# Seven half-size products for one more chunk's first product, under a new instruction order

## The chip, the cores and the metric

The kernel runs on one core of a Trainium2 chip. The metric is the device time of one execution in microseconds, and the median of three runs is given.

The names of the engines are those of the profile: PE is TensorE (matmuls; PEld its weight loads), ACT ScalarE, DVE VectorE, POOL GpSimd and SP SyncE.

## The reference

Attention with a causal mask and 16 beacon keys that every query sees, then two dense products with a squared relu between them.

```python
# q, k, v: (8, 8, 576, 64); beacon_k, beacon_v: (8, 8, 16, 64)
k_all = np.concatenate([beacon_k, k], axis=2)
v_all = np.concatenate([beacon_v, v], axis=2)
scores = scale * np.matmul(q, k_all.transpose(0, 1, 3, 2))
causal[:, Nb:] = np.triu(np.ones((S, S), dtype=bool), k=1)
scores = np.where(causal, -1000000000.0, scores)
a = np.exp(scores - scores.max(-1, keepdims=True))
a /= a.sum(-1, keepdims=True) + 1e-09
attn_out = np.matmul(a, v_all)
x = attn_out.transpose(0, 2, 1, 3).reshape(B * S, H * D)   # (4608, 512)
h = x @ w_in                                               # w_in: (512, 2048)
r = np.maximum(h, 0.0)
out = (r * r) @ w_out                                      # w_out: (2048, 512)
```

## The kernel before

**Attention.** It goes batch by batch (8 batches), four pairs of heads each. `qk` operations multiply queries by keys into PSUM (line 680 for batches 2 to 7, 687 for 0 and 1; the two heads of a pair sit on 64 rows each), ACT takes the exponential (792; 709 in batch 0), DVE sets masked places to zero (815), `av` multiplies by the values and a column of ones (837), and DVE divides by the sum (854 and 856) into `xn`, tokens by rows. The result is transposed into `xT`, a ring of 1728 tokens, by TensorE (905) for batches 0 to 2 and by DMAs from SP (`xt` operations, line 888, five to a batch) for the others. Keys, queries and values of later batches are loaded by POOL's queue (`ld`, 391; 425 and 445 for queries) and transposed by DMAs from SP (`tr`, 459).

**The dense part.** It goes in 9 chunks of 512 tokens, which don't end where batches do. The first product of a chunk is plain for chunks 0 to 6: for each of 16 tiles of 128 outputs, four matmuls over the 512 inputs (1139), or eight where the chunk crosses the end of the ring. ACT or DVE takes the relu out of PSUM (1154, 1156) and one of them squares (1164, 1166). The second product is plain for chunk 0 (1189) and is made of seven products of half-size blocks for the others (1248), whose sums and differences DVE makes (1220) and whose results are put together on the way out (347, 349, 1271).

**Chunks 7 and 8** make the first product of seven half-size products too (`add_first_both`, line 969). Tokens are split into even and odd, inputs and outputs into halves. POOL copies the chunk out of `xT` (`pull`, by line 349), DVE makes four differences of blocks of x (`xsum`, 996) and once four sums and differences of blocks of `w_in` (`asum`, 963). For each half of the outputs, products 1, 6, 7 and 4 add up in one PSUM strip (the "x" chain); after each of the first three the strip's running sum is copied to a kept area (`hold`, operations `c1`, `u2`, `u3`, by 347), and after the fourth its relu is taken (`c21`, 1038). Products 2, and 5 and 3, go to single PSUM banks in two parts each, and DVE adds the kept sums to them (`plus`, 1063). Then come relus (1087, 1089) and squares (1093, 1095). The kept areas are a pool `held` of five: three lie in the staging area `stg` of the loads, two in the buffer `pt` of attention weights. Chunk 7's copy of x lies in `qk_area`, chunk 8's in `pt`.

**Order.** No scheduler decides the order at run time. `add` registers operations with their dependencies, and `Order.run` issues them in the order of the text SEQUENCE; each word is an operation, with `@A`, `@D` or `@P` where its engine is a choice. Each engine works through its own list in that order, POOL's and SP's DMA issues too. PSUM banks (`ps`, 4), strips (2), kept areas (`held`) and staging areas (`stg`) are handed out in that order as well. `fill` operations are 12 products of an identity matrix (564), whose results nobody reads, spread over the first microseconds.

`s1.j.t.0` is tile t of the plain first product of chunk j, and `s1.j.h.n` product n of half h in the seven-product form; `s2.j.n.t` is part t of product n of the second product. `qk16.2` is a visit of the score products of batch 4, `av15.0.1` the second head of pair 15 (batch 3).

Of the kernel before, what the change touches and what calls it, by code (L numbers as in the profile page):

```python
# [16 lines left out]
ident fldq0 bkl0 fldq1 fldk0 tri fill0 warm fldk1 fill11 fldk2 fldq2 fldk3 bkc0 fldq3 sld0k1.0 tpb0 fill5 ekb0 fck0@A  # L17
fcq0@D fill2 sld0q1.0 bkl1 fcq1@D fill6 sld0k1.2 tp0.0.0k fck1@D fill8 ek0.0.0@A sld0q1.2 fill4 tpg0.0.0k tp0.0.1k
fcq2@A ld0v0 fill9 ek0.0.1@A fck3@D fill3 fck2@D tp0.0.0q tp0.0.1q fill1 eq0.0.0@A fcq3@D ld0v1 eq0.0.1@A tp0.0.3k
tpg0.0.1q tp0.0.3q ek0.0.3@A qk1.0.0 eq0.0.3@A tpg0.0.3k tpg0.0.0q tpg0.0.1k ld0v2 qk0.0.0 tp0.0.2q exp1.0.0 tp0.0.2k  # L20
fill10 two0.1.0k@D two0.1.1k@P eq0.0.2@A qk3.0.0 exp0.0.0 ld0v3 two0.1.1q@D ek0.0.2@A mask0.0.0 tp0.1.1q exp3.0.0
tpg0.0.2k tpg0.0.2q tpg0.0.3q tp0.1.1k mask1.0.0 qk2.0.0 ld0v4 two0.1.0q@D tp0.1.0k ek0.1.1@A eq0.1.1@D tp0.1.0q
exp2.0.0 tpg0.1.1k ek0.1.0@D win0 qk1.1.1 eq0.1.0@A two0.1.3k@D tpg0.1.0k tpg0.1.1q two0.1.2k@D exp1.1.1 mask2.0.0
qk0.1.2 tpg0.1.0q tp0.1.2k win2 two0.1.3q@D fill7 mask3.0.0 exp0.1.2 tp0.1.3q qk0.1.0 bkc1 tp0.1.3k ek0.1.2@D win1
exp0.1.0 qk1.1.0 eq0.1.3@D tpb1 ek0.1.3@D win3 exp1.1.0 tpg0.1.3q av0.0.0 qk0.1.1 ekb1 two0.1.2q@D tpg0.1.3k av1.0.0
norm0.0.0 sld1k0.0 exp0.1.1 qk3.1.0 norm1.0.0 sld1q0.0 xtp0.0.0 av3.0.0 exp3.1.0 qk1.1.2 norm3.0.0 av2.0.0 exp1.1.2
sld1k0.2 norm2.0.0 tp0.1.2q qk3.1.1 mask0.1.1 xte0.0.0@A sld1q0.2 xtp0.0.2 mask0.1.0 qk3.1.2 exp3.1.1 mask1.1.1
av0.1.0 eq0.1.2@D exp3.1.2 mask3.1.1 tpg0.1.2q tpg0.1.2k mask1.1.0 xtp0.0.1 qk2.1.1 xte0.0.1@D ld1v0 xte0.0.2@A
xtp0.0.3 mask3.1.0 qk2.1.0 exp2.1.1 norm0.1.0 av3.1.0 exp2.1.0 qk2.1.2 norm3.1.0 av1.1.0 xte0.0.3@A exp2.1.2 mask2.1.1
mask2.1.0 xtp0.1.3 s1.0.1.0 xte0.1.3@D av2.1.0 norm1.1.0 relu0.1.0@A s1.0.0.0 norm2.1.0 s1.0.10.0 relu0.0.0@A xtp0.1.0  # L30
sq0.0.0@D xtp0.1.2 s1.0.11.0 relu0.10.0@D ld1v1 xte0.1.2@D s1.0.7.0 xte0.1.0@D relu0.11.0@D s1.0.6.0 relu0.7.0@D
xtp0.1.1 s1.0.4.0 relu0.6.0@A xte0.1.1@D s1.0.9.0 relu0.4.0@D s1.0.1.1 relu0.9.0@A ld1v2 sq0.3.0@A s1.0.7.1
relu0.1.1@D s1.0.14.1 relu0.7.1@D s1.0.15.1 relu0.14.1@A s1.0.2.0 ld1v3 two1.0.0k@D s1.0.6.1 relu0.15.1@D relu0.2.0@A
s1.0.13.0 two1.0.1k@D relu0.6.1@A sq0.7.1@D s1.0.12.0 sq0.5.0@A ld1v4 two1.0.0q@D tp1.0.0k relu0.13.0@A relu0.12.0@D
tp1.0.0q ek1.0.0 s1.0.8.0 eq1.0.0@A s1.0.0.1 two1.0.1q@D sq0.3.1@A wout0 tpg1.0.0k tpg1.0.0q qk4.2 two1.0.2k@D
relu0.0.1@A sq0.6.0@D tp1.0.1q relu0.8.0@D exp4.2.0.0.0 s1.0.14.0 eq1.0.1@D s1.0.11.1 wout1 relu0.14.0@A tp1.0.1k
tpg1.0.1q relu0.11.1@A tp1.0.2k exp4.2.1.0.0 ek1.0.1 two1.0.3k@P s1.0.10.1 s1.0.4.1 ek1.0.2 relu0.10.1@A qk4.4 wout2
sq0.5.1@D tpg1.0.2k tpg1.0.1k s1.0.2.1 mask4.0.0 exp4.4.1.0.0 two1.0.2q@P relu0.4.1@D s1.0.8.1 relu0.2.1@D s1.0.3.0
exp4.4.0.0.0 s1.0.9.1 wout3 relu0.3.0@D s1.0.5.1 relu0.9.1@D relu0.8.1@A ldq2.0 s1.0.5.0 sq0.1.0@A mask4.0.1 s1.0.12.1
mask4.0.2 relu0.5.1@A relu0.5.0@D ld2v0 sq0.0.1@A av4.0.0 sq0.2.0@D relu0.12.1@A s1.0.3.1 norm4.0.0 sq0.4.0@A av4.0.1  # L40
two1.0.3q@P relu0.3.1@D tp1.0.2q s1.0.13.1 norm4.0.1 eq1.0.2@A s1.0.15.0 ld2v1 sq0.4.1@D relu0.13.1@A tpg1.0.2q
tp1.0.3k sq0.1.1@A relu0.15.0@D qk5.7 ek1.0.3 ldq2.1 sq0.6.1@A s2.0.0.0 sq0.2.1@D exp5.7.-1.1.0 tpg1.0.3k exp5.7.0.0.0
tp1.0.3q s2.0.2.0 exp5.7.1.0.0 s2.0.0.1 exp5.7.-1.0.0 mask5.0.1 s2.0.2.1 mask5.0.2 eq1.0.3@A mask5.0.0 wsum1 tpg1.0.3q
qk7.13 s2.0.0.2 zero2 exp7.13.-1.1.0 sq0.7.0@A av5.0.0 exp7.13.-1.0.0 ld2k0 s2.0.2.2 norm5.0.0 exp7.13.1.0.0 wsum2
av5.0.1 ld2k1 exp7.13.0.0.0 s2.0.2.3 mask7.0.2 ld2k2 norm5.0.1 s2.0.0.3 join2.1@D qk6.10 zero3 ev0.0@A ev0.2@A
s2.0.1.0 ld2k3 exp6.10.1.0.0 xtp1.0.0 exp6.10.1.0.1 ldq2.r s2.0.1.1 exp6.10.-1.0.0 mask7.0.0 mask7.0.1 exp6.10.-1.1.0
s2.0.3.0 ldq3.0 xte1.0.0@A mask6.0.0 exp6.10.0.0.0 ldq3.1 av7.0.0 s2.0.3.1 ldq3.r mask6.0.1 mask6.0.2 s2.0.1.2
norm7.0.0 ldq4.0 av6.0.0 ld2k4 av7.0.1 norm6.0.0 s2.0.1.3 join2.2@P norm7.0.1 av6.0.1 ldq4.1 join2.3@D xtp1.0.3
norm6.0.1 s2.0.3.2 xte1.0.3@D join3.3@P xtp1.0.2 xtp1.0.1 xte1.0.2@A s2.0.3.3 join3.1@D join2.0@P xte1.0.1@D s1.1.7.0
wsum3 tr2q s1.1.1.0 relu1.7.0@A join3.2@P ev0.3@A s1.1.4.0 relu1.1.0@A wsum4 joined3.1 joined2.0 joined2.1 s1.1.0.0  # L50
relu1.4.0@D s1.1.10.0 join3.0@D tr2k relu1.0.0@D joined3.0 s1.1.6.0 relu1.10.0@D sq1.0.0@A s1.1.5.0 join4.0@D ldq4.r
join4.3@D s1.1.11.0 relu1.5.0@A join4.2@D relu1.6.0@D ldq5.0 s1.1.13.0 relu1.11.0@A sq1.3.0@D ld2v2 s1.1.12.0
sq1.5.0@D relu1.13.0@A ld3k0 s1.1.15.0 qk8.4 relu1.15.0@D ld2v3 s1.1.14.0 relu1.12.0@D exp8.4.0.0.0 ld2v4 s1.1.2.0
sq1.6.0@D exp8.4.1.0.0 ld3k1 relu1.14.0@D relu1.2.0@A qk8.2 sq1.7.0@D ld3k2 s1.1.8.0 sq1.2.0@D exp8.2.0.0.0 ld3k3
s1.1.3.0 sum1.1.1 exp8.2.1.0.0 ld3k4 relu1.8.0@D s1.1.9.0 relu1.3.0@A mask8.0.0 mask8.0.2 qk9.7 mask8.0.1 relu1.9.0@A
sq1.1.0@D ev0.1@A av8.0.0 sq1.4.0@D exp9.7.-1.0.0 st0 s2.1.1.0 exp9.7.-1.1.0 sum1.2.1 st1 exp9.7.0.0.0 av8.0.1
sum1.1.0 tr3q s2.1.2.0 norm8.0.1 exp9.7.1.0.0 exp9.7.1.0.1 norm8.0.0 s2.1.1.1 mask9.0.0 qk10.10 sum1.2.0 ev1.c1.None@A
sum1.3.0 s2.1.2.1 exp10.10.-1.1.0 mask9.0.1 exp10.10.1.0.0 mask9.0.2 s2.1.6.0 tr3k sum1.3.1 ev1.c11.None
exp10.10.0.0.0 av9.0.0 s2.1.6.1 norm9.0.0 mask10.0.1 av9.0.1 ev1.u2.None@A mask10.0.2 xtp2.0.0 norm9.0.1 s2.1.7.0
xte2.0.0@A join5.0@P exp10.10.-1.0.0 qk11.13 ldq5.1 sum1.4.1 mask10.0.0 s2.1.5.0 ldq5.r exp11.13.-1.0.0 sum1.4.0  # L60
exp11.13.0.0.0 av10.0.0 ldq6.0 s2.1.5.1 exp11.13.-1.1.0 ld4k0 exp11.13.1.0.0 mask11.0.0 xtp2.0.1 s2.1.7.1 norm10.0.0
xte2.0.1@A mask11.0.1 ld4k1 qk12.2 mask11.0.2 ev1.u3.None@A av11.0.0 ld4k2 ev1.c22.None exp12.2.1.0.0 av10.0.1
norm11.0.0 s2.1.4.0 ldq6.1 exp12.2.0.0.0 norm10.0.1 ld4k3 av11.0.1 s2.1.3.0 norm11.0.1 ld3v0 xtp2.0.2 xtp2.0.3
xte2.0.2@D s2.1.3.1 xte2.0.3@D ld3v1 s1.2.13.0 ev1.c12.None ld3v2 join4.1@D s1.2.4.0 join5.2@D ld3v3 relu2.13.0@D
# [142 lines left out]
def kernel(  # L207
# [12 lines left out]
    B, H, S, D = q.shape  # L220
# [5 lines left out]
    NT = 5  # L226
# [10 lines left out]
    def sb(name, shape, dt):  # L237
        return pool.tile(shape, dt, name=name)

    FAST = 1  # L240
    BOTH = 7
    NSTG, NPT, RB = 6, 3, 3
    PW = 1664
    RING = RB * S
# [108 lines left out]
    cast = {}  # L353
# [615 lines left out]
    def add_first_both(j, G, sq):  # L969
# [6 lines left out]
        if j == BOTH:  # L976
            add_a_sums()
# [429 lines left out]
```

## Time and profile before

| | |
|---|---|
| Median of three runs | 326.29 us (324.04 to 327.10) |
| The profiled execution | 323.4 us, of which 321.7 us is the span from its first to its last instruction |
| TensorE (PE) busy | 312.7 us, 97% of the span, 3520 matmuls |
| Weight loads (PEld) busy | 230.3 us, 72% |
| DVE, ACT, POOL busy | 240.6 us (75%), 211.4 us (66%), 112.1 us (35%) |
| Plain first products, line 1139 | 640 matmuls, 104.2 us busy |
| Seven-product form of chunks 7 and 8, line 1016 | 224 matmuls of 256 columns |

How to read it: matmuls are pipelined, so a group's mean duration is longer than the time from one start to the next. What a stretch of work costs on TensorE is read from the chain in order of time, which lists the pieces that follow each other without a gap, or from the starts in the timeline. The windows give, for a stretch, the busy time of PE, PEld, DVE, ACT and POOL in this order.

### The profile page before, as it was taken

How to read it: one execution, taken by the hardware profiler on the slowest of the kernel's cores; microseconds unless marked ns; L12 is line 12 of the kernel's file. 1: busy time of each engine (PE TensorE's matmuls, PEld its weight loads, DVE VectorE, ACT ScalarE, POOL GpSimd, SP SyncE). 2: the span in 40 equal slices, each digit the busy share in tenths (PEclk: the TensorE clock that was granted, in tenths of full speed). 3: DMA queues.
4: the chain of work that ended last, by engine and by line, in shares of the span. 5: the costliest groups of instructions: out<-in, count | busy, mean ns of one | idle time of the engine just before them, and what ended most of it. 6: DMA issues, size and time to landing. Idle time of an engine off the chain costs nothing.

```text
span 321.7 us, 8494 instructions
## 1 busy us (share of the span) xinstructions
PE 312.7 (97%) x3520; PEld 230.3 (72%) x3520; DVE 240.6 (75%) x538; ACT 211.4 (66%) x318; POOL 112.1 (35%) x159
## 2 busy tenths in 40 slices
PE   6899999999999999999999999999999999999995
PEld 2468765644886468888786568665887788888884
DVE  3788875688975796856875788778866687989882
ACT  3994987357893787685856685477762686586610
POOL 7934767738089239177440050000000600000000
PEclk9999999999999999999999999999999999999999
DMA  7999999999999999999998989040231600030033
GB/s 156 148 203 200 154 204 149 164 163 137 201 172 155 216 163 149 136 180 120 186 138 144 235 82 163 18 142 3 49 29 30 176 2 0 3 130 2 2 147 114
DMA packets 135934, 39.93 MB, mean 124 GB/s; under 512 B 117336, under 2 KB 131544, under 8 KB 135896
## 3 DMA queue, kind: packets, MB, share of 16 engines
q0 software_dynamic: 84928, 18.10, 73.1%
q1 hardware_dynamic: 50314, 20.93, 30.9%
q8 instruction: 27, 0.44, 0.6%
q10 hardware_dynamic: 654, 0.38, 0.4%
q14 instruction: 11, 0.09, 0.1%
HBM read 37.22 MB, written 9.44 MB: 145 GB/s over the span
## 4 chain that ended last, share of the span: by engine, by line
PE 95%; DVE 2%; ACT 1%; DMA 1%; issue 0%; DVEq 0%; ACTq 0%
PE ps L1139 31%; PE ps L1248 29%; PE ps L837 9%; PE strip L680 5%; PE ps L1189 4%; PE strip L1016 4%; PE ps L1016 3%; PE strip L1248 2%; PE ps L680 2%; PE strip L687 2%; PE ps L905 1%; PE ps L529 1%; PE ps L564 1%; DMA stg<-in_beacon_k_dram 1%; ACT pt L709 0%; DVE g L349 0%
## 5 line engine op out<-in xcount | busy, mean ns | idle before, releaser
L1139 PE MATMUL ps<-xT,w_in 128*128 128x512 bf16 (+6 forms) x640 | 104.2, 315 | 0.0
L1139 PEld LDWEIGHTS <-w_in 128*128 128x128 bf16 x640 | 56.9, 98 | 34.6 <-issue 1.6
L792 ACT ACTIVATE pt<-strip 128x1024 bf16<-128x1024 f32 (+3 forms) x77 | 70.5, 958 | 5.5 <-PE strip L680 5.0
L1154 ACT ACTIVATE g<-ps 128x512 bf16<-128x512 f32 (+2 forms) x77 | 42.1, 558 | 34.8 <-PE ps L1139 32.3
L1248 PEld LDWEIGHTS <-g 128*128 128x128 bf16 x512 | 48.4, 98 | 8.0 <-issue 1.2
L1248 PE MATMUL ps<-w_out,g 128*128 128x256 bf16 x352 | 44.9, 273 | 0.0
L1156 DVE TENSOR_SCALAR g<-ps 128x512 bf16<-128x512 f32 (+2 forms) x51 | 30.2, 603 | 14.1 <-PE ps L1139 13.7
L1248 PEld LDWEIGHTS <-sum_area 128*128 128x128 bf16 x384 | 36.5, 98 | 5.7 <-issue 1.3
L815 DVE TENSOR_TENSOR pt<-pt,tri 128x512 bf16<-128x512 bf16 (+1 forms) x93 | 30.7, 356 | 12.7 <-ACT pt L792 11.3
L837 PEld LDWEIGHTS <-pt 128*128 128x128 bf16 x930 | 35.2, 99 | 6.2 <-issue 1.3
L837 PE MATMUL ps<-vb,pt 128*128 128x65 bf16 x930 | 37.8, 195 | 0.4 <-DVE qT L349 0.4
L391 POOL DMA_DIRECT2D vb<-in_v_dram x40 | 34.2, 876 | 7.5 <-DMA w_in<-in_moe_w_in_dram 6.6
L856 DVE TENSOR_TENSOR xn<-ps,rcp 128x320 bf16<-128x320 f32 (+2 forms) x64 | 31.5, 492 | 2.2
L1166 DVE TENSOR_TENSOR g<-g 128x1024 bf16<-128x1024 bf16 (+2 forms) x42 | 27.2, 662 | 5.6 <-ACT g L1154 5.2
L347 ACT COPY osb<-ps 128x512 f32<-128x512 f32 x27 | 15.7, 587 | 23.4 <-PE ps L1248 21.3
L1248 PE MATMUL ps<-w_sum,sum_area 128*128 128x256 bf16 x240 | 30.8, 273 | 0.2 <-ACT osb L347 0.2
L792 ACT ACTIVATE pt<-ps 128x512 bf16<-128x512 f32 x42 | 24.5, 604 | 8.3 <-PE ps L680 7.6
L391 POOL DMA_DIRECT2D qk_area<-in_k_dram x30 | 25.9, 881 | 4.3 <-DMA w_out<-in_moe_w_out_dram 3.8
L854 DVE RECIPROCAL rcp<-ps 128x5 f32<-128x5 f32 (+2 forms) x64 | 12.1, 189 | 17.8 <-PE ps L837 17.3
L349 POOL COPY qk_area<-xT 128x512 bf16<-128x512 bf16 x4 | 2.8, 747 | 56.4 <-DMA xT<-xn 56.4
L1164 ACT ACTIVATE g<-g 128x1024 bf16<-128x1024 bf16 (+2 forms) x22 | 19.2, 882 | 3.9 <-DVE g L1156 3.7
L1271 DVE TENSOR_TENSOR osb<-ps,osb 128x512 f32<-128x512 f32 (+1 forms) x26 | 16.8, 648 | 6.6 <-PE ps L1248 3.0
(105 smaller groups left out, 421.1 us busy)
## 6 DMA issues: line engine op xcount, KB each, us to landing
out_dram<-osb SPq DMA_DIRECT2D x16, 512.0 KB, 3.3
vb<-in_v_dram POOLq DMA_DIRECT2D x24, 128.0 KB, 5.6
stg<-in_q_dram POOLq DMA_DIRECT2D x12, 256.0 KB, 4.8
qk_area<-in_k_dram POOLq DMA_DIRECT2D x18, 128.0 KB, 5.2
w_in<-in_moe_w_in_dram POOLq DMA_DIRECT2D x4, 512.0 KB, 10.5
w_out<-in_moe_w_out_dram POOLq DMA_DIRECT2D x4, 512.0 KB, 10.3
vb<-in_v_dram POOLq DMA_DIRECT2D x8, 112.0 KB, 6.0
qk_area<-in_k_dram POOLq DMA_DIRECT2D x6, 112.0 KB, 5.0
```

Of the source, the lines that this page charges most:

```text
L391: insts.append(nc.gpsimd.dma_start(out=dst[lo:rows], in_=t[b, :, t0:t0 + rows - lo, :].transpose([1, 0, 2])))
L680: nc.tensor.matmul(out, keys[hp, c, pr], rhs, start=True, stop=True)
L792: nc.scalar.activation(out, in_, AF.Exp, bias=0.0, scale=scale)
L815: nc.vector.tensor_tensor(out=d, in0=d, in1=tri[0:rows, m0:m0 + m, 0:w][:, None].to_broadcast([rows, 2, m, w]), op=ALU.min)
L837: nc.tensor.matmul(a[0:w, at + (t - tl[0]) * (D + 1):at + (t - tl[0] + 1) * (D + 1)], P[0:rr, hj, o:o + w], vb[b % 2][0:rr, c, 2 * pr + hj ...
L856: nc.vector.tensor_tensor(out=xn[b % 2].rearrange("p t (h d) -> p h t d", d=D)[:, h0:h0 + nh, tl[0]:tl[0] + nt], in0=a[:, :, :, 0:D], in1= ...
L1016: nc.tensor.matmul(o[:, i % 2 * HT:(i % 2 + 1) * HT], lhs[:, m, f * 128:(f + 1) * 128], rhs[:, m], start=fresh and i % 2 == 0 and m == 0, ...
L1139: nc.tensor.matmul(h[:, lo - spans[0][0]:hi - spans[0][0]], w_in_sb[:, mc, ft * 128:(ft + 1) * 128], xT[:, mc, lo % RING:lo % RING + hi - lo],
L1154: nc.scalar.activation(dst, h, AF.Relu, bias=0.0, scale=1.0)
L1156: nc.vector.tensor_scalar(out=dst, in0=h, scalar1=0.0, scalar2=None, op0=ALU.max)
L1166: nc.vector.tensor_tensor(out=d, in0=d, in1=d, op=ALU.mult)
L1248: nc.tensor.matmul(o, lhs[:, f, t * 128:(t + 1) * 128], rhs[:, f], start=fresh and f == 0, stop=f == HF - 1, skip_group_check=True)
```

## The change

The first product of chunk 6 takes the seven-product form (`BOTH` from 7 to 6). Chunks 6 and 8 now copy x into `qk_area`, chunk 7 into `pt`. Since batch 7's attention still uses `pt` when chunk 6 begins, an operation without instructions (`grab`) takes the two kept areas in `pt` first, and another (`ptfree`) gives them back after batch 7's last `av`; the first copies wait for the loads that use `stg` (`stg_free`) instead of for attention. In chunk 6 the second half's use of kept areas and banks is tied to the first half's additions (`old`), and the x chain no longer waits for all of batch 7's scores and exponentials. Chunk 6's operations are registered only with the last batch. The whole of SEQUENCE is new, from the first word to the last; the words below show three places of it (the start, the transposes of batch 3 and the copies for chunk 6).

```diff
 SEQUENCE = """
-ident fldq0 bkl0 fldq1 fldk0 tri fill0 warm fldk1 fill11 fldk2 fldq2 fldk3 bkc0 fldq3 sld0k1.0 tpb0 fill5 ekb0 fck0@A
-fcq0@D fill2 sld0q1.0 bkl1 fcq1@D fill6 sld0k1.2 tp0.0.0k fck1@D fill8 ek0.0.0@A sld0q1.2 fill4 tpg0.0.0k tp0.0.1k
+ident fldq0 bkl0 fldq1 fldk0 tri fill10 warm fldk1 fill4 fldk2 fill3 fldq2 fill6 fldk3 fill2 bkc0 fldq3 fcq0@A
+sld0k1.0 fill7 fill1 fck0@D sld0q1.0 tpb0 tp0.0.0q tp0.0.0k sld0k1.2 fill5 eq0.0.0@D fck1@A fcq1@D tpg0.0.0q ek0.0.0@D
...
-mask17.0.0 xt3.2 s2.2.4.0 sum2.4.0 exp16.2.0.0.0 join6.1@D s2.2.5.1 xt3.0 mask16.0.0 mask16.0.1 qk17.8 ev2.c22.None
-xt3.1 s2.2.4.1 exp17.8.-1.1.0 exp17.8.0.0.0 av16.0.0 ev2.c21.None@D tr5q s2.2.3.0 exp17.8.-1.0.0 exp17.8.1.0.0
+joined4.1 joined5.1 join6.0@D av15.0.1 joined6.0 exp16.2.1.0.0 s2.2.5.1 norm15.0.1 mask16.0.0 s2.2.4.0 xt3.3
+mask16.0.1 ev2.c22.None qk17.8 mask17.0.0 xt3.0 s2.2.3.0 exp17.8.-1.0.0 exp17.8.-1.1.0 av16.0.0 xt3.1 exp17.8.0.0.0
+mask17.0.2 s2.2.4.1 norm16.0.0 mask17.0.1 av16.0.1 xt3.2 ev2.c21.None@A av17.0.0 exp17.8.1.0.0 norm16.0.1 s2.2.3.1
...
+norm25.0.0 pull6.1.3072 av25.0.1 mask26.0.1 qk27.13 pull6.0.3072 norm25.0.1 av26.0.0 exp27.13.0.0.0 ld7v0 s2.4.3.1
+norm26.0.0 exp27.13.1.0.0 s2.4.4.1 ev4.c12.None pull6.2.3072 ld7v1 mask27.0.2 s1.5.10.0 mask27.0.1 mask27.0.0
...
 """
...
     FAST = 1
-    BOTH = 7
+    BOTH = 6
...
     order = Order(
-        pools={"strip": range(2), "held": range(5), "ps": range(4), "stg": range(NSTG)},
+        pools={"strip": range(2), "held": (3, 4, 0, 1, 2), "ps": range(4), "stg": range(NSTG)},
     )
...
+    stg_free = []
...
-        exps = [o for q in last for o in qk_ops[q]] + [x[0] for q in last for x in exps_of[q]]
         if j == BOTH:
             add_a_sums()
+            grab = add("grab", "-", 0.0, None, take=("held", 2))
+            add("ptfree", "-", 0.0, None, deps=probs, give=[(grab, 0, "held"), (grab, 1, "held")])
+            stg_free.extend(cast[B - 1, x, c] for x in "qkv" for c in range(NT))
...
+        sums = None
         for half in range(2):
+            old = sums if j == BOTH else None
...
-                        deps=deps + done_g + (exps if chain == "x" else []),
+                        deps=deps + done_g + (old["c11"] if old and chain != "x" else []),
...
-            hold("c1", 1, None, probs)
+            hold("c1", 1, None, stg_free + (old["c11"] if old else []))
...
-            hold("u2", 6, None, [])
+            hold("u2", 6, None, old["c22"] if old else [])
...
-            hold("u3", 7, None, [])
+            hold("u3", 7, None, old["c12"] if old else [])
...
         if b >= 1:
-            for j in late:
-                add_chunk(j)
-            late = []
+            while late and (late[0] < BOTH or b == B - 1):
+                add_chunk(late.pop(0))
```

## The prediction

> **What bounds the kernel now.** I read the page first, then the chain in order of time, the windows, the timelines of TensorE and SyncE, and the rows of single lines.
>
> ```profile
> span 321.7 us, 8494 instructions
> PE 312.7 (97%) x3520; PEld 230.3 (72%) x3520; DVE 240.6 (75%) x538; ACT 211.4 (66%) x318; POOL 112.1 (35%) x159
> ...
> PE   6899999999999999999999999999999999999995
> ```
>
> TensorE is busy in every slice but the first two and the last. Nine microseconds are idle, and the windows place them:
>
> ```profile
> 0.00:12.00 12.00, 8.53 (x53) 3.79 (x53) 4.75 (x18) 6.84 (x16) 10.20 (x22) 1.00 1.09 159
> 12.00:24.00 12.00, 10.38 (x189) 6.90 (x186) 11.07 (x36) 11.64 (x19) 7.21 (x11) 1.00 2.04 179
> ...
> 240.00:276.00 36.00, 36.00 (x386) 29.87 (x385) 26.45 (x50) 21.63 (x30) 6.01 (x8) 1.00 0.19 47
> 276.00:300.00 24.00, 24.00 (x222) 21.50 (x221) 21.93 (x41) 16.86 (x20) 0.00 (x0) 1.00 0.12 45
> ```
>
> The columns after the length are PE, PEld, DVE, ACT and POOL. Up to 24 us the softmax chain of batch 0 sets the pace (ACT 11.64 and DVE 11.07 of 12 us). From there on TensorE is full. So a microsecond of matmul removed after 24 us is a microsecond of span, unless the new order makes TensorE wait. What the two forms of a first product cost is in the chain in order of time (start, us, what):
>
> ```profile
> 60.44 0.86 PE ps L1189 x4
> ...
> 244.58 10.48 PE ps L1139 x96
> 255.06 0.87 PE strip L1016 x8
> 255.94 1.75 PE ps L1139 x16
> ...
> 258.20 1.75 PE strip L1016 x16
> ```
>
> L1139 at 244 us is the plain product of chunk 6. L1016 is the seven-product form of chunks 7 and 8.
>
> **Part 1, the matmuls of chunk 6.** Removed: 16 tiles of four 128-row steps. Chunk 6 (tokens 3072 to 3583) crosses the end of the xT ring at 3456, so each step is two matmuls of 384 and 128 columns, 128 in all. 96 of them take 10.48 us, 0.1092 us each, so 128 take 13.97. Added: 7 products x 2 halves x 4 x 2 = 112 matmuls of 256 columns, at 0.87/8 = 0.109 us, 12.21 us. The difference is **-1.76 us**, on the path. Sixteen weight loads go too; PEld is at 29.87 of 36 us there and bounds nothing.
>
> One rule was weighed. A pair of 384 and 128 columns takes 0.218 us in the row above, and one matmul of 512 columns (L1189, the second product of chunk 0) 0.86/4 = 0.215, so the cut costs next to nothing. The Trainium skill (TensorE: Matmul & The Clock Gate, Back-to-back issue gap) gives about 81 ns as the sustained spacing of 128-column matmuls that each load weights. By that the plain form would cost 64 x (0.162 + 0.081) = 15.6 us and the saving would be 3.3 us. The row shows no such floor, so the sum keeps 1.76.
>
> **Part 2, what the new form asks of the other engines.** Removed on ACT and DVE: 16 relu evacuations (603 ns on ACT, 687 on DVE) and 8 squares (0.70 to 1.06 us), together about 17 us. Added by the rows of chunks 7 and 8: 8 copies or relus out of a strip at 1.01 us, 12 additions at 0.684, 8 relus at 0.54 on average (L1087 and L1089), 8 squares at 0.875 (L1093 and L1095), 4 differences at 0.42 (L996): 8.1 + 8.2 + 4.3 + 7.0 + 1.7 = 29.3 us. That is 12.5 us more. In 240 to 276 us the two engines are busy 48.1 of 72 us; with 12.5 more in some 34 us they are at 60.6 of 68, 89%. The nearest row is 276:300, where the same form runs at 38.8 of 48 us with DVE at 91%, and TensorE is busy 24.00 of 24.00. So I cost it at **0**. The cover is the matmuls between two products on the same strip. If it were gone, each of the 8 strip products would wait up to a copy (1.01 us), 8 us in all; that is the far end.
>
> On POOL eight copies of xT (747 to 840 ns per 512 tokens) move ahead, and the loads of v for batch 7 now stand between and behind them. Four of the copies wait for xT of batch 6, so ld7v3 and ld7v4 wait with them, and av28 waits for those loads. From av27's last product that takes: its normalisation 1.4, two transposing DMAs 2.5 plus at most 6.0 to landing, two copies and a load issue 2.3, the last load's 5.6 (median of vb loads), 17.8 us at most. In the changed order 14 tiles of chunk 5's first product and six half products of its second lie between (20 x 0.87 = 17.4 us), and three score visits besides, some 2 us. Covered, by little only at the longest landing: **0**.
>
> **Part 3, the order.** Every engine's list is new. Score visits (L680, 64 rows) each cost about 0.1 us on the way in and out; from batch 1 on there are 35 in both orders, so nothing is gained there. In the start four visits fewer are made (10 against 14), where TensorE isn't the bound. The start's softmax work is the same on ACT and DVE, which leave 0.36 and 0.93 us idle in 12 to 24 us; I take **0** for the start, between -2.5 (half of its 5.1 us idle) and +1.5 (a second gap like the one of 1.48 us shown below).
>
> The one step that the lists show tighter is chunk 3's first product, which waits for the transposed x of batch 3:
>
> ```profile
> 129.69 0.49 DVE L856 TENSOR_TENSOR xn<-ps,rcp 128x320 bf16<-128x320 f32 x1
> 130.21 3.80 SPq L888 DMA_TRANSPOSE xT<-xn  x3
> 137.58 1.05 PE L1139 MATMUL ps<-xT,w_in 128*128 128x192 bf16 x8
> ...
> DMA to landing us min/median/max: 4.1/5.0/6.0
> ```
>
> The normalisation ends at 130.18, three DMAs go out in 3.80 us, and the product starts at 137.58, 7.40 us after. The last line is those three's time to landing; the last one landed at 132.75 + 4.1 = 136.9, 0.7 us early. In the new order SyncE issues a fourth DMA ahead of them (xt3.3, which chunk 3 doesn't need), so the last needed one starts 3 x 1.27 = 3.8 us after the normalisation. TensorE has less to do until then: of the work between av15.0.1 and the product one half product (0.87) and one score visit (0.65) are gone and two av (0.47 each) come in, so 6.8 us remain. All 25 such DMAs land in 2.3/3.0/6.0 us (min/median/max). The wait is thus 3.8 + 2.3, 3.0 or 6.0 - 6.8: none, 0.0 or 3.0 us. The landing time fell from 6.0 to 4.1 in the burst shown, so I take 3.4 for a fourth: **+0.4 us**, bounds 0 and 3.0. Behind it on SyncE stand the transposes of batch 5, needed much later.
>
> **Sum.** -1.76 + 0 + 0 + 0 + 0.4 = -1.4 us on the profiled execution (323.4 us, of which 321.7 are span): 322.0. The median of the runs shown is 326.29, 2.9 above that execution, and the change touches nothing that I can see of this spread. So I forecast 326.29 - 1.4 = **324.9 us**. About 1%, 3.3 us, is what a measurement of this kernel can tell from no change (its own three runs span 3.1 us).
>
> **Rivals.**
>
> *Slower: the strip copies become a wait.* In the new order some strip products are only three short products apart (3 x 0.44 = 1.31 us), and the way from the end of one to the next is a matmul's tail of 0.16 plus the copy's 1.01 plus some 0.1 of hand-over, 1.27. One square (1.06 us on ACT) ahead of a copy turns the 0.04 into a wait. It decides from 0.22 us late per copy (8 x 0.22 = 1.76); at 0.7 us it costs 5.6 and the time is 326.3 - 1.8 + 5.6 = 330.1. For it: ACT carries most copies, and batch 7's softmax ends just before. Against: chunks 7 and 8 pass 16 such copies without a gap.
>
> *The late transposes.* If the landing is 6.0 us, the wait is 3.0 and the time 324.9 + 2.6 = 327.5. For: SyncE's burst shares the engines with POOL's loads (queue q0's packets take 73.1% of the span). Against: in the new order POOL's loads before the burst are issued earlier relative to it.
>
> *Faster: an earlier full clock.* TensorE's first matmuls run at half speed:
>
> ```profile
> 1.43 1.03 PE L564 MATMUL ps<-ident 128*128 128x512 bf16 x2 [1.43 <-POOL ident masks.py:199]
> 3.95 0.27 PE L476 MATMUL ps<-ident,bks 16*128 16x16 bf16 x4 [1.48 <-DVE bks L469]
> 4.15 1.46 PE L564 MATMUL ps<-ident 128*128 128x512 bf16 x3
> ...
> 7.91 0.47 PE L564 MATMUL ps<-ident 128*128 128x512 bf16 x1
> ```
>
> One 512-column fill lasts 0.47 us at 7.91 where three last 1.46 at 4.15 (0.43 apart): the matmuls go twice as fast from about 8 us on, 4 us after the end of the gap of 1.48 us. The page's clock row shows 9 from the start, so only the durations tell this. The new order has seven fills in a row from 1.43, so no such gap stands before the first copy. If that came 3 us sooner, the work of 5 to 8 us would take half, 1.5 us less, and with up to 1 us from a better filled start the time would be 324.9 - 2.5 = 322.4. The Trainium skill (TensorE: Matmul & The Clock Gate, What's actually happening) says that the gate looks at free-running windows of about 3.4 us and opens after a busy one; the 8 us here fit that, and by it the gain would come or not with the window's phase. Against the rival: in this stretch TensorE mostly waits for DVE and ACT, which a faster clock doesn't help.
>
> *No gain.* Short new waits, scattered over the list, take the 1.8 us: 326.3.
>
> **How the numbers follow.** Forecast 0.48, strip copies 0.15, late transposes 0.10, early clock 0.20, no gain 0.07. The forecast's own range is 323.4 to 326.4. The wider range reaches to 320.8 (the early clock, with the spread of the runs) and to 329.5 (the copies at 0.6 us each). Faster by over 1% (under 323.0) comes from the early clock and a little of the forecast: 0.25. Slower by over 1% (above 329.6) from the copies, and the transposes with another wait beside them: 0.17. Within 1%: 0.58.
>
> **What would show it.** Right: L1139 loses 128 matmuls, L1016 has 336 instead of 224, the first product of chunk 6 takes 12.2 us of TensorE, and from 24 us on TensorE's windows are full. Part 2 is wrong if TensorE shows idle time before L1016 ended by ACT or DVE, or before L837 ended by vb's loads. Part 3 is wrong if TensorE sits idle near 140 us until xT lands for more than 1 us, or if the first window moves by over 1 us. The whole is wrong if the waits of TensorE after 24 us sum to more than 2 us.

## The result, and the profile after

The kernel after takes 327.77 us (median of 21 runs, 325.26 to 332.0), the kernel before 324.23 us (median of 21 runs beside them). The ratio is 1.008, 95% interval 1.0056 to 1.0105: about 2.6 us slower, where 1.4 us faster was forecast. (The two medians are 3.5 us apart; the ratio leaves out executions over 1.5% above their kernel's fastest.) The time lies inside the range given; the direction is wrong.

The profiled execution took 328.52 us, with a span of 326.8; before it was 321.7, so the change costs 5.1 us there. From the page of the kernel after:

```profile
span 326.8 us, 8474 instructions
...
PE 312.6 (96%) x3489; PEld 233.3 (71%) x3504; DVE 246.4 (75%) x553; ACT 222.8 (68%) x325; POOL 112.2 (34%) x161
...
PE   6899999998989999989999999999999999999995
...
PEclk9679999999999999999999999999999999999999
```

TensorE is no busier than before (312.6 against 312.7 us), and the idle time has grown by the 5 us. The busy row shows where: an 8 at three places of the first half (the slices from 73.5, 89.9 and 138.9 us) that were 9 before, and nothing from there to the end. (Fifteen of the 3504 matmuls have no record, hence x3489.) And the clock row, which was full from end to end before (it counts the slow first microseconds as full), dips in the second and third slice.

The timeline of TensorE gives the places (start, us busy, what, idle before and what ended it):

```profile
66.75 9.66 PE L1147 MATMUL ps<-xT,w_in 128*128 128x512 bf16 x43
...
77.72 0.65 PE L683 MATMUL strip<-qT,kT 64*128 64x352 bf16 x12 [1.31 <-DMA kT<-qk_area]
...
91.33 1.03 PE L1256 MATMUL ps<-w_sum,sum_area 128*128 128x256 bf16 x8 [1.53 <-ACT osb L350]
...
145.90 3.32 PE L1147 MATMUL ps<-xT,w_in 128*128 128x320 bf16 x28 [1.55 <-DMA xT<-xn]
```

The first line is chunk 1's first product. Before, it started at 64.11 us, so 2.64 us are lost by then:

```profile
64.11 9.66 PE L1139 MATMUL ps<-xT,w_in 128*128 128x512 bf16 x44
```

Three waits follow, 4.39 us together: for the transposed keys of batch 2, for an evacuation to `osb`, and for the transposed x of batch 3. The chain in order of time says why the evacuation was late:

```profile
84.87 0.59 ACT osb L350
...
85.47 5.12 DMA out_dram<-osb
...
90.69 0.59 ACT osb L350
```

The copy at 84.87 is `ev0.1`, the last of chunk 0's results. Only then can `st0` store them, and the store takes 5.12 us to land. `ev1.c1` at 90.69 writes the same buffer and has to wait for it. In the kernel before, `st0` was issued at 80.58 us, 4.9 us sooner, and landed after 3.4 us:

```profile
84.02 0.59 ACT L347 COPY osb<-ps 128x512 f32<-128x512 f32 x1 [0.59 <-DMA out_dram<-osb]
```

The distance is much the same in both: ACT is ready for `ev1.c1` 2.9 us after the end of `ev0.1` there and 3.1 us after it here. So it is the landing, 1.7 us longer, that makes the wait, and not the later issue. The store took 5.0 to 6.9 us in runs two, three, nine and twelve below, which have the new order at this place, and 3.4 in runs seven and eight, which have the old one. What lengthens it was not tried.

The end of the kernel is as forecast. The windows (length, then busy time of PE, PEld, DVE, ACT and POOL, the clock, DMA) cover the whole of chunk 6's new form, from its first product at 246.99 us:

```profile
230.00:250.00 20.00, 20.00 (x252) 16.47 (x251) 17.09 (x37) 14.50 (x21) 0.00 (x0) 1.00 0.14 28
250.00:260.00 10.00, 10.00 (x137) 9.15 (x136) 8.71 (x19) 6.37 (x7) 1.18 (x3) 1.00 0.21 39
260.00:280.00 20.00, 20.00 (x186) 17.92 (x184) 19.26 (x36) 17.30 (x22) 3.88 (x6) 1.00 0.20 65
280.00:300.00 20.00, 20.00 (x186) 17.94 (x184) 17.34 (x32) 16.10 (x19) 0.00 (x0) 1.00 0.15 54
```

DVE is at 19.26 of 20 us and ACT at 17.30, and still TensorE never waits. From the starts of the matmuls, the plain first product of chunk 6 took 3.64 us (64 of 128 columns) and 10.40 us (64 of 384), 14.04 in all. The seven-product form went from 224 matmuls in 24.46 us to 336 in 36.68, so chunk 6 takes 12.22. That is -1.82 us.

So the account of the profiled execution is +2.64 (the start) + 4.39 (three waits) - 1.82 (chunk 6) = +5.2 us, against 5.1 measured.

### The profile page after: what moved, and what is told of

It reads as the page before. It is cut to its first block, busy times and chain, and to the rows that moved or that the text cites. A ratio compares the mean times of both kernels' runs of the same rounds, so it can differ in the third digit from the quotient of the medians.

```text
span 326.8 us, 8474 instructions
## 1 busy us (share of the span) xinstructions
PE 312.6 (96%) x3489; PEld 233.3 (71%) x3504; DVE 246.4 (75%) x553; ACT 222.8 (68%) x325; POOL 112.2 (34%) x161
## 4 chain that ended last, share of the span: by engine, by line
PE 83%; DMA 7%; DVE 4%; SPq 2%; ACT 1%; issue 1%; DVEq 0%; ACTq 0%
PE ps L1256 26%; PE ps L1147 22%; PE ps L840 8%; PE strip L1024 6%; PE ps L1024 5%; PE strip L683 4%; PE ps L1197 4%; DMA osb<-in_q_dram 2%; PE strip L1256 2%; DMA kT<-qk_area 2%; PE strip L690 2%; DMA out_dram<-osb 2%; DMA xT<-xn 2%; PE ps L683 1%; SPq L462 1%
## 5 line engine op out<-in xcount | busy, mean ns | idle before, releaser
L1147 PE MATMUL ps<-xT,w_in 128*128 128x512 bf16 (+3 forms) x501 | 88.3, 325 | 2.5 <-DMA xT<-xn 1.5
L1147 PEld LDWEIGHTS <-w_in 128*128 128x128 bf16 x512 | 47.2, 98 | 33.6 <-DMA xT<-xn 1.7
L1162 ACT ACTIVATE g<-ps 128x512 bf16<-128x512 f32 (+2 forms) x70 | 36.3, 532 | 24.1 <-PE ps L1147 23.2
L1256 PE MATMUL ps<-w_out,g 128*128 128x256 bf16 x352 | 45.2, 273 | 0.0
L1164 DVE TENSOR_SCALAR g<-ps 128x512 bf16<-128x512 f32 (+2 forms) x42 | 25.8, 622 | 17.2 <-PE ps L1147 17.0
L1174 DVE TENSOR_TENSOR g<-g 128x1024 bf16<-128x1024 bf16 (+2 forms) x34 | 20.9, 630 | 8.6 <-ACT g L1162 7.9
L352 POOL COPY qk_area<-xT 128x384 bf16<-128x384 bf16 (+2 forms) x12 | 6.9, 600 | 48.5 <-DVE rcp L857 41.4
L350 ACT COPY osb<-ps 128x512 f32<-128x512 f32 x24 | 14.3, 594 | 13.1 <-PE ps L1256 10.9
L683 PEld LDWEIGHTS <-kT 64*128 64x128 bf16 x432 | 13.9, 96 | 10.7 <-issue 6.6
```

The costliest lines, as they stand in the source:

```text
L683: nc.tensor.matmul(out, keys[hp, c, pr], rhs, start=True, stop=True)
L1147: nc.tensor.matmul(h[:, lo - spans[0][0]:hi - spans[0][0]], w_in_sb[:, mc, ft * 128:(ft + 1) * 128], xT[:, mc, lo % RING:lo % RING + hi - lo],
L1162: nc.scalar.activation(dst, h, AF.Relu, bias=0.0, scale=1.0)
L1164: nc.vector.tensor_scalar(out=dst, in0=h, scalar1=0.0, scalar2=None, op0=ALU.max)
L1174: nc.vector.tensor_tensor(out=d, in0=d, in1=d, op=ALU.mult)
L1256: nc.tensor.matmul(o, lhs[:, f, t * 128:(t + 1) * 128], rhs[:, f], start=fresh and f == 0, stop=f == HF - 1, skip_group_check=True)
```

## The experiments

The theory after reading the two traces: chunk 6 brings its 1.8 us; the new order loses more than that, in the start, where the clock falls back, and in three late transfers. The first rival: the waits are only where a shortage of ACT, DVE or DMA comes to light, and would move on if they were removed. The second: chunk 6's form is not worth its extra work.

### One: the three transfers moved

```diff
-relu1.6.0@A qk8.4 join4.3@D join4.0@D s1.1.10.0 ld3k1 join4.1@D exp8.4.0.0.0 relu1.11.0@D s1.1.2.0 ld3k2 relu1.10.0@D exp8.4.1.0.0
+relu1.6.0@A ev0.1@A st0 st1 join4.3@D join4.0@D s1.1.10.0 ld3k1 join4.1@D relu1.11.0@D s1.1.2.0 qk8.4 exp8.4.0.0.0 exp8.4.1.0.0 ld3k2 relu1.10.0@D
...
-mask8.0.0 ev0.1@A sq1.4.0@D qk9.7 st0 mask8.0.2
+mask8.0.0 sq1.4.0@D qk9.7 mask8.0.2
...
-mask9.0.1 st1 ev1.c11.None
+mask9.0.1 ev1.c11.None
...
-s2.2.4.0 xt3.3 mask16.0.1
+s2.2.4.0 mask16.0.1
...
-xt3.2 ev2.c21.None@A
+xt3.2 xt3.3 ev2.c21.None@A
```

> The kernel after, with three places of its order changed and nothing else: xt3.3 is issued behind xt3.2 instead of ahead of xt3.0; ev0.1, st0 and st1 are issued ahead of qk8.4 (st1 stood behind tr3q); qk8.4 and its two exponentials are issued behind s1.1.2.0, two tiles later. Theory (the order's three late transfers are what made it slower): TensorE's waits of 1.31 us at 76 us (kT), 1.53 us at 90 us (the copy that waits for a store) and 1.55 us at 144 us (xT of batch 3) go; of the last 0.3 us stays, since one DMA issue ahead of three is 1.27 us. -1.3 - 1.5 - 1.3 = -4.1 us against the kernel after, 323.6 us by its median of 327.77, about that of the kernel before (0.998 to 1.002 of it). Rival 1 (the waits only move on, to the next thing that is late on ACT, DVE or SyncE): less than 1.5 us gained, over 326.2. Rival 2 (the new form of chunk 6 costs more than it saves): the three waits go, but the end of the run, from 250 us on, is where the time is lost, and the kernel stays 1% behind the one before.

Measured: 333.18 us, ratio 1.0209 (1.0154 to 1.0264). Slower still by over 1%. All three waits are gone from the trace, and one that is longer than their sum stands in their place, with 6.83 us of half clock (a granted clock of 0.50) behind it:

```profile
91.19 0.21 PE L840 MATMUL ps<-vb,pt 80*128 80x65 bf16 x1 [6.19 <-DMA vb<-in_v_dram]
```

The queues of POOL and of SP show what it waited for:

```profile
78.86 0.75 POOL L394 DMA_DIRECT2D vb<-in_v_dram  x1
```

```profile
77.38 7.77 SPq L462 DMA_TRANSPOSE qT<-qk_area  x1
```

This is `ld2v4`, the last part of batch 2's v. It landed 12.3 us after its issue; in the kernel after, it was issued at 78.89 and took 4.8 us. What differs is SP: the transposes of batch 3's queries (`tr3q`) stand behind `st0`, which had kept them until 86.07. With the store out of the way they started at 77.38, and the load issued 1.5 us behind them crawled. The late store had been what kept transposes and loads apart. Rival 1 holds here.

### Two: more fills in the start

Five more fill products where TensorE was idle for 1.30 us.

```diff
-qk0.0.0 eq0.0.2@D ld0v1 fcq3@D tpg0.0.2q tpg0.0.1k
+qk0.0.0 eq0.0.2@D ld0v1 fcq3@D tpg0.0.2q fill12 fill13 fill14 fill15 fill16 tpg0.0.1k
```

> The kernel after, with five more fill products between the score product qk0.0.0 and the transposes tp0.0.3q, where TensorE was idle for 1.30 us at 7.6 us; nothing else. Theory (the idle time in the stretch from 7.5 to 10.95 us is why the clock record shows half clock from 10.95 to 21.19 us): the clock stays full from about 4 us on, the granted clock of a run is 1.00 instead of 0.98, and the time is 2 to 2.6 us lower than the kernel after's, 325.5 us by its median of 327.77. Rival 1 (the half clock comes from too little work after 10.95 us, or at random): the clock stays at 0.98 and the time within 0.5 us of 327.8. Rival 2 (the start is bound by DVE and ACT whatever the clock): the clock is 1.00 and the time doesn't fall by more than 0.5 us.

Measured: 327.34 us, ratio 1.0067 (1.0025 to 1.0108). In the profiled execution the clock is 1.00 to the end and the span 324.0. But only 4 of the 12 runs had full clock (a mean of 0.998 or more), and it came at 7.38 us in the profiled one, 4.12 in the kernel after, so that one execution does not tell the fills from the chance of when it comes. And chunk 1's first product starts at 66.78 us in it, no sooner than in the kernel after. The full clock had won 1.37 us by 24 us, and lost it again by 42. One line of DVE's timeline shows where:

```profile
35.42 3.12 DVE L352 COPY w_sum<-qk_area 96x768 bf16<-96x768 bf16 x2
```

The pair takes 0.69 us elsewhere. POOL copied between the same two areas meanwhile:

```profile
36.16 0.84 POOL L352 COPY w_sum<-qk_area 96x768 bf16<-96x768 bf16 x1
...
37.66 1.55 POOL L352 COPY w_sum<-qk_area 96x768 bf16<-96x768 bf16 x1
```

The lower span comes later, from kT (0.18 us of wait left) and xT (none, with the same order of SP's queue there). The theory's gain is not shown by the times, and for the start the second rival holds, as far as one execution shows.

### Three: the old start in front of the new order

The first 410 words are those of the kernel before; the other words follow in the new order. At the seam, where one order passes into the other:

```diff
 join3.1@D join2.0@P xte1.0.1@D
-s1.1.7.0 wsum3 tr2q s1.1.1.0
+ld2v2 join3.0@D ev0.3@D s1.1.4.0
```

> The first 410 words of the old order (the start and batch 1, up to the copies of chunk 1's x, 64 us) in front of the rest of the new order; the program is that of the kernel after, chunk 6 in seven products. Theory: chunk 1's first product starts at 64.1 us as in the kernel before (66.75 in the kernel after), which gives -2.6 us, the clock stays full; the transposes of batch 2's keys are out some 4 us sooner, so the wait of 1.31 us at 76 us goes too; the waits at 90 and at 144 us stay. -2.6 - 1.3 = -3.9 us against the kernel after, 323.9 us by its median. Rival (the start is not where time is lost, its delay is taken up later by cover): under 1 us gained, 326.8 or more.

Measured: 327.35 us, ratio 1.0035 (0.9997 to 1.0073), some 1.4 us better than the kernel after by the two ratios. The profiled execution does what was expected (span 322.5, chunk 1's first product at 64.27, no wait at 76 us, 1.78 us for `osb` at 86, none for xT; 0.64 us for batch 3's kT at 97 are new), but the median keeps little over a third of it. Three of the 12 runs had full clock, at a median of 324.22 us; the median of the other nine was 327.73.

### Four and five: chunk 6 with the old order up to it

The old order's first 917 words, then its first 974, each followed by the rest of the new order, with chunk 6 in seven products. The two seams:

```diff
 tr6q mask22.0.0 qk22.11
-norm21.0.0 ev3.c21.None@A s1.4.5.0 exp22.11.0.0.0
+grab exp22.11.0.0.0 exp22.11.-1.1.0 exp22.11.1.0.0
...
 relu4.15.0@D s1.4.8.0 sq4.7.0@D
-exp24.5.-1.1.0 exp24.5.-1.0.0 sum4.1.1
+grab st7 s1.4.9.0 sum4.1.1
```

> The first 917 words of the old order (through chunk 3's second product, some 190 us) in front of the rest of the new order, with chunk 6 in seven products: the change of chunk 6 by itself, without the new start and without the three places with the late transfers. Theory (the first step of the forecast holds: 128 matmuls of 13.97 us become 112 of 12.21 us, and the added copies, sums and relus are covered): 1.76 us less than the kernel before, 322.5 us by its median of 324.23, ratio 0.9945, and no wait of TensorE over 0.3 us after 250 us. Rival (the extra 12.5 us on ACT and DVE are not covered): no gain or a loss, 324 us or more, with idle time ahead of the strip products.

> As the run with 917 old words, but the old order is kept for its first 974 words (into chunk 4's first product, about 200 us), so that the seam lies where the two orders differ by few operations and by no exponential. In the run before, the seam itself made two waits for the exponentials of batch 5 (0.96 and 1.01 us at 173 us) and a stretch of half clock behind them. Theory (chunk 6's form gains 1.76 us and costs no wait): at full clock the span is 321.7 - 1.76 = 319.9 us, the time 321.6; by the median of the kernel before, ratio 0.9945. Rival (the saving of 16 matmuls isn't there, or the extra work on ACT and DVE takes it back): the span at full clock stays over 321 us and TensorE is idle after 250 us.

Measured: ratios 1.0024 (0.9974 to 1.0073) and 0.9998 (0.9971 to 1.0025). Neither shows the gain, and both show the seam instead: two waits for ACT's exponentials (0.96 and 1.01 us at 173 us) in the first, 0.69 and 0.38 us for ACT's relus at 190 us in the second. The first one is worth a look, since the clock answered. Its windows:

```profile
172.44:175.85 3.41, 1.44 (x27) 0.89 (x24) 0.25 (x2) 2.97 (x5) 0.00 (x0) 1.00 1.19 126
175.85:179.26 3.41, 3.19 (x13) 1.36 (x13) 2.34 (x6) 1.78 (x2) 0.00 (x0) 0.50 0.72 225
179.26:182.68 3.42, 3.37 (x54) 2.23 (x53) 2.88 (x9) 0.25 (x1) 0.00 (x0) 1.00 0.91 233
```

TensorE was idle for 1.97 of 3.41 us, and the 3.41 us behind it were granted half clock. So the waits of 1.97 us cost another 1.7, half of 3.41.

### Six: the load that was late, moved as well

Run one, with `ld2v4` issued behind `ld2v3`.

```diff
-joined3.1 ld2v3 relu1.15.0@A
+joined3.1 ld2v3 ld2v4 relu1.15.0@A
...
-s1.1.14.0 ld2v4 sq1.5.0@D
+s1.1.14.0 sq1.5.0@D
```

> The kernel with the three places changed (333.18 us), and one load more moved: ld2v4, the last part of batch 2's v, is issued behind ld2v3, ahead of the loads of batch 3's keys. In that run TensorE waited 6.2 us for this load, which was issued at 78.86 us and took 12.3 us to land; the transposes of batch 3's queries had started at 77.38 instead of 86.07 us, since no store stood in their way any more. Theory (the transposes hold up the load that is issued behind them): issued at about 75.5 us it lands before 82 us, the wait of 6.2 us goes, and with it the two windows of half clock behind it (up to 3.4 us): 324 to 325.5 us, ratio to the kernel before 0.996 to 1.001. Rival (the early transposes hold up the other loads of batch 3 as well, and these make the next wait): over 328 us, with TensorE waiting for kT or qT of batch 3 near 100 us.

Measured: 330.26 us, ratio 1.0185 (1.0143 to 1.0226). The wait for vb is gone and TensorE waits 3.53 us for batch 3's kT at 98 us. The rival holds again: the loads of batch 3's keys are held up by the same early transposes, which started at 77.75 us; loads of 128 KB of keys took 9.2 us to landing (median), 4.5 in the kernel after.

### Seven: the new start in front of the old order

The kernel before, with the new order's first 413 words. At the seam:

```diff
 xte1.0.2@D join3.1@D join2.2@D
-s1.1.4.0 joined3.0 joined2.0 wsum3
+s1.1.7.0 wsum3 tr2q s1.1.1.0
```

> The kernel before (chunk 6 in the plain form) with the first 413 words of the new order in front of the rest of its own: the new start by itself. Theory (the new start is worth a loss of its own, by the clock that falls back): chunk 1's first product starts 2.6 us later than in the kernel before (66.7 instead of 64.1 us), the mean granted clock of most runs is 0.98 to 0.99, and the time is 2 to 2.6 us over the kernel before, ratio 1.006 to 1.008. Rival (the delay is taken up behind the start, or the clock of the kernel before falls back as often): within 0.7 us of it, ratio under 1.002.

Measured: 326.62 us, ratio 1.0052 (1.0021 to 1.0084), about 1.7 us slower. The new start costs time by itself. The profiled execution, the second fastest of the ten, does not show the 2.6 us that were expected of it: chunk 1's first product starts at 64.66 us, 0.55 later than before, with 3.41 us of half clock. With run three the two halves add up: 0.52% for the new start and 0.35% for all the rest of the new order, chunk 6 included, are 0.87%, against 0.80% for the whole change.

### Eight: a seam that costs nothing

The old order for 1038 words (to the scores of batch 6, about 215 us). At the seam:

```diff
 s2.4.5.0 xt5.2 sum4.4.1
-qk26.11 mask25.0.1 ev4.u3.None@D s2.4.5.1
+grab asum1 ev4.u3.None@A qk26.11
```

> Chunk 6 in seven products with the old order kept for its first 1038 words (to the scores of batch 6, about 215 us), where the two orders differ only by the loads of v for batch 7, which the old one issues earlier. The seam at 974 words had cost 1.07 us of waits for ACT at 190 us; this one should cost none. Theory (the form of chunk 6 is worth what its matmuls say, 14.04 us before and 12.23 us in the kernel with the seam at 974): at full clock the span is 321.7 - 1.8 = 319.9 us, and the ratio to the kernel before 0.9945; from 250 us on TensorE has no wait over 0.3 us. Rival (the gain is taken back by copies and sums, or by the earlier loads): ratio over 0.998.

Measured: 322.65 us, ratio 0.9939 (0.9904 to 0.9974). By the two ratios it beats both kernels, by 0.6% and 1.4%. Its span is 321.1 us. The windows, with chunk 6's new form from 241.02 us on:

```profile
230.00:250.00 20.00, 20.00 (x296) 17.50 (x291) 17.02 (x42) 12.95 (x17) 0.00 (x0) 1.00 0.01 2
250.00:270.00 20.00, 20.00 (x186) 17.91 (x184) 18.89 (x34) 16.97 (x19) 5.01 (x8) 1.00 0.30 84
270.00:300.00 30.00, 30.00 (x278) 26.89 (x276) 25.71 (x46) 24.68 (x30) 0.00 (x0) 1.00 0.10 36
```

The profiled execution has 6.83 us of half clock in its start (chunk 1's first product at 65.20 us, 1.09 later than before) and is 0.6 us shorter all the same. Chunk 6's saving is shown, and its cover too, together with whatever the new order from 215 us on adds to it.

### Nine and twelve: the new middle mended behind the old start

Run three with `ev0.1` and `st0` issued earlier (the store went out 4.0 us sooner) and `xt3.3` behind `xt3.2`; then the same with `ld2v4` sooner.

```diff
-s1.1.9.0 exp8.2.1.0.0
+s1.1.9.0 ev0.1@A st0 exp8.2.1.0.0
...
-ld2v3 relu1.15.0@A
+ld2v3 ld2v4 relu1.15.0@A
```

> The first 410 words of the old order in front of the new one, as before, with two more places changed: ev0.1 and st0 are issued ahead of the exponential exp8.2.1.0.0, about 3 us sooner, and xt3.3 behind xt3.2. Theory (of the new order's loss the head, one store and one transpose are all that matters): the wait of 1.78 us for the store at 86 us goes, and the span at full clock falls from 322.5 to 320.1 to 320.8 us; ratio to the kernel before 0.995 to 0.997. Rival (the transposes of batch 3's queries stand behind this store in SyncE's queue, start sooner with it, and hold up the loads of batch 3 again): a wait of 2 us or more for vb or kT between 84 and 100 us, ratio 1.003 or more.

> The last one (first 410 old words, ev0.1 and st0 three microseconds sooner, xt3.3 behind xt3.2) with ld2v4 issued behind ld2v3 as well, ahead of the loads of batch 3's keys. There TensorE had waited 2.25 us at 82 us for this load, issued at 77.50 us, just ahead of the transposes at 78.27, and landed 6.7 us later; 3.41 us of half clock came behind. Theory (only this load was too late for the sooner transposes): issued at about 74.5 us it lands by 80, the wait and the half clock go, and at full clock the span is 323.3 - 2.25 - 1.7 = 319.4 us; ratio to the kernel before 0.992 to 0.995. Rival (the transposes hold up the key loads of batch 3 next, as when the same load was moved in the other order): TensorE waits over 1 us for kT near 97 us, ratio over 0.998.

Measured: ratio 0.998 (0.9941 to 1.002), then 1.0002 (0.9966 to 1.0038). In the first, `tr3q` started at 78.27 us, just behind the issue of `ld2v4` at 77.50, and there is the rival's wait, followed by 3.41 us of half clock:

```profile
84.26 0.21 PE L840 MATMUL ps<-vb,pt 80*128 80x65 bf16 x1 [2.25 <-DMA vb<-in_v_dram]
```

In the second that wait, kT's and xT's are all gone from the trace, and from 42 to 318 us TensorE is never idle: from chunk 1's first product to the end it is 255.6 us, against 257.6 in the kernel before. Its profiled execution lost 3.96 us before that product, to a start with 1.52 us of idle time in one window, 13.65 us of half clock and a wait of 1.34 us for DVE's copies at 36 us. The median did not fall as the trace of the middle says it should; what the other runs waited for stays open.

### Ten and eleven: a pause of TensorE, by itself

```diff
-s2.6.1.0 h7.0.c110
+s2.6.1.0 fill12 pause fill13 h7.0.c110
...
+spot = qT[0][:, 0, 0:512]
+nc.tensor.matmul(ps[...], ident, spot, start=True, stop=True)   # fill12, fill13
+for _ in range(2):                                              # 8 in the long one
+    nc.gpsimd.memset(spot, 0.0)
```

> The kernel before, with a pause of TensorE put in where it is full (behind s2.6.1.0, about 268 us): one product that reads a buffer no longer used, two memsets of that buffer on POOL, and a product that reads it again. TensorE is idle for the two memsets and the way there and back, about 1.3 us, and has 0.43 us more work. Theory (the clock falls back only if a window of 3.41 us holds more than 1.55 to 1.8 us of idle time): +1.7 us, the clock behind the pause stays full. Rival (any pause of over a microsecond costs a window of half clock): +3.4 us, and half clock for 3.41 us behind it.

> The same with eight memsets: TensorE is idle for about 4.1 us and has 0.43 us more work. Theory (windows of 3.41 us; one with too much idle time is followed by one at half clock): half clock for one or two windows behind the pause, 3.41 or 6.83 us, in which half the work is done, so +1.7 or +3.4 us besides the 4.5 us: +6.2 to +7.9 us. Rival (the clock falls back in the start only, where ACT and DVE have work for TensorE to wait on): +4.5 us and full clock.

Measured: 325.25 us, ratio 1.0028 (0.999 to 1.0065), and 331.6 us, ratio 1.022 (1.0171 to 1.0269): by the ratios 0.9 us more (-0.3 to 2.1) and 7.1 us more (5.5 to 8.7). In the profiled executions the same matmuls behind the pause come 1.81 us later than ahead of it in the short one (1.22 us idle, full clock throughout), and 7.34 us later in the long one (4.72 us idle):

```profile
262.32:265.73 3.41, 1.33 (x12) 0.95 (x10) 0.70 (x2) 2.73 (x3) 1.84 (x4) 1.00 0.00 0
265.73:269.15 3.42, 0.78 (x3) 0.40 (x3) 0.00 (x0) 0.00 (x0) 2.36 (x5) 0.50 0.00 0
269.15:272.56 3.41, 3.41 (x18) 2.35 (x16) 2.71 (x5) 0.00 (x0) 0.00 (x0) 0.50 0.02 5
272.56:275.97 3.41, 3.41 (x34) 3.04 (x32) 2.26 (x5) 2.77 (x4) 0.00 (x0) 1.00 0.00 0
```

Full clock is back one whole busy window after the pause. The idle time and the two products make 5.15 us; of the other 2.2, 2.1 are half of the 4.2 us of work, from 268.37 to 272.56, that ran at half speed. The theory holds on both sides of the limit.

## Why the prediction was wrong

**Part 1, the matmuls of chunk 6: right.** -1.76 forecast, -1.82 measured, and run eight shows it in the time.

**Part 2, nothing for the extra work of ACT and DVE: right.** No wait for a strip copy, in the kernel after or in run eight, with DVE at 19.26 of 20 us. The slower rival with 5.6 us for these copies is refuted.

**Part 3, "I take 0 for the start": the step that failed first.** The bounds were -2.5 and +1.5. Run seven puts it at +1.7 (0.7 to 2.7 by its interval); the profiled executions show +2.64 in the kernel after and +0.55 in run seven. The step counted the busy time of ACT and DVE, and that is nearly the same: up to chunk 1's first product 45.2 and 45.3 us before, 46.6 and 45.9 after. It put no price on the clock falling back, nor on what meets in the start. In the kernel after the clock was at half for 10.24 us; in run two it was full, and DVE's copies beside POOL's took the time instead. How much of the 1.7 us is which was not tried apart and stays open.

**Part 3, "The one step that the lists show tighter": the step that failed most.** By the ratios of runs three and eight, which differ by 0.96%, the new order between the start and 215 us costs some 3.1 us (an estimate, 1.4 to 4.8 by the two intervals). With 1.7 for the start and -2.0 for run eight the stretches make +2.8, against +2.6 measured.

In the profiled execution three waits stand there, where one was named. That one was sized at +0.4 with bounds of 0 and 3.0 and cost 1.55 us. The term that was mis-sized is the fourth transpose's time to landing: 3.4 us were taken, it took 5.10 (from 140.66 us), and 3.3 and 2.7 in runs two and three, where with the same four DMAs in the same order there was no such wait.

The two that were missed cost 1.31 us (kT) and 1.53 us (the store, which landed after 5.12 us instead of 3.4). For kT, the transposes were issued at 71.19 us instead of 66.07: the late start makes 2.6 of these 5.1 us, and the queries' transposes ahead of them waited for DVE's copies until 66.96 us. The prediction compared SP's queue for the transposes of x, but followed neither these nor a store to the evacuation that writes its buffer next. That the three waits make up the middle's loss in the median is not shown: run twelve's trace has none of them, and its ratio of 1.0002 is below run three's by 0.33%, within the intervals of both.

**The early clock: the mechanism came, the gain did not.** Full clock came at 4.12 us instead of 8.08, as that rival said. It was granted for two windows and lost for three. In the four other profiled executions with the new start it came at 4.14 to 7.38 us, in the eight others with the old start at 6.55 to 9.93; it then fell back in four of the five with the new start and in four of the nine with the old. In the kernel after:

```profile
7.53:10.95 3.42, 1.67 (x15) 0.51 (x13) 2.42 (x9) 2.22 (x5) 3.42 (x4) 1.00 1.61 175
10.95:14.36 3.41, 3.29 (x29) 1.93 (x30) 2.13 (x7) 2.38 (x5) 3.41 (x6) 0.50 2.83 150
...
17.78:21.19 3.41, 3.31 (x41) 2.27 (x41) 2.79 (x10) 3.26 (x5) 0.92 (x2) 0.50 1.24 206
21.19:24.60 3.41, 3.17 (x82) 2.67 (x79) 2.67 (x12) 3.07 (x5) 0.83 (x1) 1.00 1.24 206
```

The prediction took the first full clock as the end of the matter. Its own last sentence, that it would be wrong if the waits after 24 us came to more than 2 us, is what happened: 4.39.

**The starting point.** The forecast was set from a median of 326.29 of three runs; beside the kernel after, the same kernel's median of 21 runs was 324.23. The spread follows the granted clock: of 98 runs of the kernel before beside the experiments, 53 had a mean clock of 0.998 or more and a median of 323.57 us, the other 45 one of 326.07. The kernel after had such a clock in 1 of 21 runs (325.26 us), and run seven in 1 of 10 (326.52 us, no faster than its others).

**Luck.** That the measured time lies in the wide range is owed to this starting point: from 324.23 us the same working gives a forecast of 322.8 and an upper end of 327.4, and 327.77 is above it. The rival of the late transposes named 327.5, next to the time measured; but its wait was 3.0 us, and the one found is 1.55 with other losses beside it. The range's upper end of 329.5 is also 0.2 above its own sum (326.3 - 1.8 + 8 x 0.6 = 329.3).

## What to carry to other kernels

When an order is replaced, take every wait in it as a spacing that something may rely on. Here a late store had kept the transposes off the loads; with the store moved forward, the transposes held up a load, and that cost more than all the waits removed. Give each store and each transpose on the way a landing time with its spread, follow the store to the next writer of its buffer and each moved load to the transposes that will run beside it, and judge the new order by stretches (old start with new rest, new start with old rest), since a local gain of 1.8 us is easily paid for elsewhere. Keep the pauses of a full TensorE short of some 1.5 us in any 3.41: beyond that they are paid for a second time.

## What the runs showed of the hardware

**The clock.** It changes only at borders 3.41 us apart, whose position against the kernel's start differs from execution to execution. Where TensorE is otherwise full, windows with 1.53, 1.55 and 1.75 us of idle time kept full clock, and windows with 1.72, 1.97, 2.08, 2.96 and 3.41 us lost it for the next. In the start, among small products, less could be enough: 0.70 us in run eight's window from 9.76 us, while 1.16 us in run two's from 14.20 us kept it. The Trainium skill (TensorE: Matmul & The Clock Gate, HAM oscillation — how this bites in real kernels) gives as its rule that there should be no idle gap above about 3.4 us; here gaps of 0.96 and 1.01 us in one window did it (run four). By that rule the new start would have kept its clock: its longest gap was 1.44 us. And busy time alone does not bring the clock back in the start; this window of run twelve, with TensorE busy throughout at half clock by the profile, was followed by three more:

```profile
9.97:13.38 3.41, 3.41 (x29) 1.71 (x25) 2.24 (x6) 3.41 (x7) 2.67 (x5) 0.50 2.24 157
```

**Loads beside transposes.** The same load of 80 KB landed after 4.8 us when it was issued 7 us ahead of a transpose, 6.7 us when 0.8 us ahead, and 12.3 us when 1.5 us behind.

**DVE beside POOL.** DVE's copies and products between bf16 areas of SBUF took 1.4 to 2.9 us instead of 0.35 to 0.41 while POOL copied or issued loads (run two at 32.8 and 35.7 us, run four at 33.9); its copies out of PSUM beside the same work kept their 0.74. The Trainium skill (SBUF — State Buffer, SBUF: two separate sides) describes a pair of ports that either DVE or GpSimd holds for a whole instruction while the other waits; the longest of these stretches is more than one such copy of 0.84 us, so a single instruction of POOL does not explain it. Where these collisions fall differs between executions of one order, and that was not tried apart.
